# Retention and two MLPs on one core: chunks of the two sequences by turns, weights spilled in their two parts, order read from a table

## The chip, the cores and the metric

The kernel runs on one NeuronCore of a Trainium2 chip. The metric is the device time of one execution in microseconds (us), lower is better. A difference of some 0.3% is about what can be told from none. The engines are named as in the profile: PE (matmuls; PEld are its weight loads), DVE (vector), ACT (scalar), POOL (GpSimd), SP (which issues all DMAs here).

## What is computed

A retention layer (linear attention with a decay for each head) over two sequences of 768 tokens, then two MLPs over all 1536 tokens, in float32:

```python
# q, k, v: (2, 8, 768, 64)
for t in range(S):
    state = gamma * state + outer(k[:, :, t], v[:, :, t])
    y[:, :, t] = scale * q[:, :, t] @ state
x = y as (1536, 512)
h = x @ w_in                      # 512 -> 2048
P = a[0] + a[1]*h + a[2]*h**2 + a[3]*h**3
Q = 1.0 + abs(b[0])*abs(h) + abs(b[1])*h**2
x = (P / (Q + 1e-6)) @ w_out      # 2048 -> 512
h = x @ w2_in
out = (h / (1 + exp(-h))) @ w2_out
```

## The kernel before

**Parts instead of float32.** PE multiplies fp32r numbers, so each operand is held as a high part and a low part (`xh` and `xl`, `ih` and `il`, `oh` and `ol`, `gh` and `gl`), and each product is three matmuls: high by high, high by low, low by high. A weight comes in as raw words; for each unit (128 x 512) ACT makes two rows (`wt<-raw`, `raw<-raw,par`), DVE two (`wt<-wt,raw`, `wt<-raw,wt`; L371 and L373), which give the whole number in a `wt` buffer, of which there are five. From it ACT takes the high part (`ih<-wt` or `oh<-wt`, L370 in the profile), and POOL or DVE the low part (`il<-wt,ih` or `ol<-wt,oh`, L375). There are three `raw` buffers.

**Attention in twelve chunks** of 128 tokens, function `attention`. Four chunks make a token group of 512; there are three groups. The chunks stand sequence after sequence: chunks 0 to 5 are the first sequence, 6 to 11 the second, and the state `bd` goes from each chunk to the next, from one of two buffers to the other. PE makes scores (L417), the outputs (L462, and L472 from the state) and the step of the state (L450); DVE masks the scores (`am<-`) and makes `xl`; POOL multiplies keys by their decay (`kn<-kn,cst`) and queries by `gq` (`qT<-qT,gq`), which is loaded anew for ten of the chunks. All outputs of chunks 0 to 3 go through PSUM bank `h1`, so that PE's next output waits until ACT's `xh` and DVE's `xl` have read the one before.

**Steps.** A weight pair is 256 hidden features: four units of input weights and output weights in a slot. Each pair is used by two steps: 12 matmuls into a bank `h0` or `h1` (L508), an elementwise stage on ACT and DVE, a split into `gh` and `gl`, and 12 matmuls into the banks `acc` (L558). There are 96 steps: three groups by eight pairs by two, in the first MLP and in the second. Uses of a pair are counted u0 to u47, steps s0 to s95. The first MLP's elementwise stage takes six rows of DVE and five of ACT for a step, the second's one on each.

**Slots and spills.** Four slots, and two more once attention has given its memory back, hold the pairs in use. Eight pairs are needed again after their slot has gone to another: u0 to u3 come back as u20 to u23, two of the second MLP's come back as u38 and u39, two as u46 and u47. For these each whole unit goes from its `wt` to DRAM (`spill<-wt`, 32 transfers of 256 KB), comes back into a `wt` (`wt<-spill`), and is then split again by ACT (L370) and POOL or DVE (L375).

**What sets the order.** Every engine operation is recorded with a rank worked out from the numbers in `R` (due times and offsets). `Flow.order` then walks a plan with assumed durations and on each engine picks the ready operation of lowest rank; the instructions of each engine, and SP's list of DMAs, are fixed in that order. Every engine works through its list strictly in order: an instruction that waits holds all behind it, and so does a DMA on SP whose source or destination isn't ready.

Of the kernel before, what the change touches and what calls it, by code (L numbers as in the profile page):

```python
# [1 line left out]

# [5 lines left out]
F32 = mybir.dt.float32  # L8
# [11 lines left out]
R = {'T0': 321.15, 'tau0': 7.46, 'tau1': 48.5, 'c0': -178.03, 'dc': 40.95, 'conv': 16.72, 'half': 117.82, 'absl': -3.34, 'raw': 149.99, 'ret': 721.79, 'spl': 159.79, 'hi': 3.19, 'lo': -120.86, 'inn': 327.86, 'later': 56.09, 'split': 40.22, 'out': 153.78, 'evac': -230.82, 'qload': 1.4, 'scl': 120.62, 'sc': 68.71, 'am': -21.97, 'gr': 164.55, 'av': -289.58, 'bd': -408.25, 'xh': -7.59, 'xl': 65.69, 'glp': 21, 'lop1': 16, 'lop2': 24, 'scp': 0, 'ps': 18, 'ksc': 24.5, 'ka': 0, 'late': 15, 'mid': 4, 'pev': -94.54, 'pld': 38.1, 'wm': 11, 'mk': -0.34, 'ck': 14.22, 'g2': (1, 0, 2), 'lw': -276.76}  # L20
# [22 lines left out]
class Flow:  # L43
# [14 lines left out]
    def op(self, eng, dur, rank, emit, reads=(), writes=(), port=False):  # L58
        after = []
        for c in reads:  # L60
            after += c.writers
        for c in writes:
            after += c.writers + c.readers
        o = Op(eng, dur, rank, emit, list(dict.fromkeys(after)), port)
        for c in reads:
            c.readers.append(o)
        for c in writes:
            c.writers, c.readers = [o], []
        o.index = len(self.ops)
        self.ops.append(o)  # L70
        return o

    def order(self):
        free = {e: 0.6 for e in (*self.TAIL, "sync")}
        cands, done = {e: [] for e in free}, []
        port = 0.0
        landed = 0.0
        for o in self.ops:
            if not o.waits:
                cands[o.eng].append(o)  # L80
        while True:
            best = None
            for e, cs in cands.items():
                if cs:
                    at = max(free[e], min(max(o.ready, port) if o.port else o.ready for o in cs))
                    if best is None or at < best[0]:
                        best = (at, e)
            if best is None:
                break
            at, e = best  # L90
            o = min(
                (o for o in cands[e] if (max(o.ready, port) if o.port else o.ready) <= at + 1e-9),
                key=lambda o: (o.rank, o.index),
            )
            cands[e].remove(o)
            o.start = at
            if e == "sync":
                free[e] = at + self.ISSUE
                landed = max(at + self.FIRST, landed) + o.dur
                end = landed + 0.1  # L100
            else:
                free[e] = at + o.dur
                end = at + o.dur + self.TAIL[e]
            if o.port:
                port = at + o.dur
            o.end = end
            for f in o.feeds:
                f.ready = max(f.ready, end)
                f.waits -= 1
                if not f.waits:  # L110
                    cands[f.eng].append(f)
            done.append(o)
        assert len(done) == len(self.ops)
        return done
# [3 lines left out]
def retention_two_mlps(  # L118
# [104 lines left out]
    def at_chunk(c):  # L223
        return 5.5 * c if c < CPG else T0 + R["c0"] + R["dc"] * (c - CPG)

# [48 lines left out]
    bank = {n: Buf(n, [P, GT], F32, psum) for n in ("a0", "a1", "acc0", "acc1", "acc2", "acc3", "h0", "h1")}  # L274

# [56 lines left out]
    def weights(u):  # L332
        (l, p), s, old = loads[u]
        sl = slots[s]
        need = at_step[2 * u]
        for half in range(2):
            w = w_dram[l][half].bitcast(I32)
            nm = "io"[half]
            for un in range(2):
                rank = need - R["conv"] + R["half"] * half + un  # L340
                us = slice(un * UNIT, (un + 1) * UNIT)
                wt = wts()
                kept = spill.get(((l, p), half, un))
                if old:
                    dma(need - R["ret"] + half, 0.66, wt.t, kept.t, [kept], [wt])
                else:
                    raw = raws()
                    rh, rl = raw.words
                    if half == 0:
                        src = w[2 * P * un : 2 * P * (un + 1), 4 * P * p : 4 * P * (p + 1)]  # L350
                    else:
                        src = w[(2 * p + un) * P : (2 * p + un + 1) * P, :]
                    c = 2 - half
                    dst = raw.t[:].rearrange("p (c f) t -> p c (f t)", c=c)
                    dma(need - R["raw"] + half, 1.32, dst, src.rearrange("(c p) f -> p c f", p=P), [], [rh, rl])
                    wi = wt.t.bitcast(I32)
                    lo_w, hi_w = raw.t[:, :, 0], raw.t[:, :, 1]

                    act(rank - R["absl"], wt.t, hi_w.bitcast(F32), AF.Abs, [rh], [wt], more=0.03, scale=W_SCALE)

                    act(rank - R["lw"], lo_w, lo_w.bitcast(U32), AF.Identity, [lbc], [rl], ptrs=1, more=0.03, scale=L_SCALE, bias=lb)
                    stt(rank, wi, wi, 3, lo_w, ALU.logical_shift_left, ALU.bitwise_or, [rl], [wt])

                    stt(rank, wi, hi_w, -0x80000000, wi, ALU.bitwise_and, ALU.bitwise_or, [rh], [wt])
                    if kept:
                        dma(need + R["spl"], 0.66, kept.t, wt.t, [wt], [kept])
# [13 lines left out]
                op("pool" if on_pool else "dve", 1.23 if on_pool else 0.6, rank + R["lo"], lo, [wt, ch], [cl], True)  # L380


    def attention(c, s_banks, o_banks):
        b, ci = divmod(c, NCI)
# [59 lines left out]
        new = bd[c % 2]  # L444
# [53 lines left out]
    def step(s, l, g, u, j, first, last, part):  # L498
# [43 lines left out]
        for m in range(4):  # L542
# [44 lines left out]
            elif last:  # L587
# [9 lines left out]
                r0 = g * GT + m * P  # L597
# [120 lines left out]
```

## Time and profile before

| | before |
|---|---|
| median of 3 runs | 618.96 us (618.27 to 619.92) |
| the profiled execution | 618.69 us, span 616.9 us |
| PE busy | 587.8 us (95%) |
| DVE busy | 441.3 us (72%) |
| ACT busy | 388.9 us (63%) |
| POOL busy | 98.2 us (16%) |
| DMA | 71.34 MB, mean 116 GB/s |

The span is what the profiler shows from the first to the last instruction; the execution's own time lies 1.8 us above it. Matmuls are pipelined and their ends are modelled: a matmul of 512 columns shows 0.39 us, while the next begins 0.227 us later. So a busy PE is not a full one, and the stages are better judged by the number of matmuls in them.

### The profile page before, as it was taken

The numbers are of one execution on the slowest core, as the hardware profiler recorded it, in microseconds if no ns is written. First come the engines' busy times: TensorE is split into PE (matmuls) and PEld (weight loads), VectorE is DVE, ScalarE is ACT, GpSimd is POOL, SyncE is SP. The second block draws the span as 40 slices with busy tenths as digits, with TensorE's granted clock in tenths as the row PEclk, the third lists the DMA queues.
The fourth block names the chain that finished last, engine by engine and source line by source line (L and its number), as shares of the span: only waits on it lengthen the run. The fifth ranks groups of instructions, "written<-read, shape, count | busy, mean of one in ns | idle before, by whom it ended". The sixth has DMA issues, their size and how long they took to land.

```text
span 616.9 us, 8056 instructions
## 1 busy us (share of the span) xinstructions
PE 587.8 (95%) x2950; PEld 477.2 (77%) x2950; DVE 441.3 (72%) x674; ACT 388.9 (63%) x657; POOL 98.2 (16%) x80
## 2 busy tenths in 40 slices
PE   6689989999989999999999999999999999999997
PEld 6577767677768788788787877877888888888886
DVE  1788998999999999999999898985424133332321
ACT  1568878898899787879788588874333132432222
POOL 1753654455443100000000000000000000000000
PEclk8988989999989999999999999999999999999999
DMA  8996774442342211004201545684122000020001
GB/s 282 384 359 210 269 255 146 156 128 75 100 150 86 70 52 35 34 1 142 98 0 52 165 156 188 208 265 162 51 86 64 6 0 26 23 73 1 0 2 68
DMA packets 34088, 71.34 MB, mean 116 GB/s; under 512 B 3712, under 2 KB 3712, under 8 KB 34048
## 3 DMA queue, kind: packets, MB, share of 16 engines
q1 hardware_dynamic: 34048, 70.82, 34.8%
q8 instruction: 23, 0.38, 0.2%
q14 instruction: 17, 0.14, 0.1%
HBM read 58.22 MB, written 12.58 MB: 115 GB/s over the span
## 4 chain that ended last, share of the span: by engine, by line
PE 32%; DVE 15%; ACT 9%; DMA 6%; issue 3%; ACTq 0%; DVEq 0%; SPq 0%
PE acc L558 17%; PE h L508 15%; DMA raw<-in_moe_w_out_dram 3%; DMA raw<-in_moe_w_in_dram 3%; DVE wt L308 2%; DVE s L308 2%; ACT r L293 2%; DVE gl L301 2%; DVE u L308 2%; DVE r L308 1%; DVE t L308 1%; ACT w L293 1%; ACT wt L293 1%; ACT s L293 1%; ACT gh L293 1%
## 5 line engine op out<-in xcount | busy, mean ns | idle before, releaser
L508 PE MATMUL h<-xh,ih 128*128 128x512 f32 x384 | 153.6, 400 | 7.1 <-DVE s L308 5.9
L508 PE MATMUL h<-xh,il 128*128 128x512 f32 x384 | 150.8, 393 | 0.3 <-DVE il L375 0.3
L508 PE MATMUL h<-xl,ih 128*128 128x512 f32 x384 | 150.5, 392 | 0.0
L301 DVE TENSOR_TENSOR gl<-w,gh 128x512 fp32r<-128x512 f32 x48 | 33.2, 691 | 104.4 <-ACT gh L293 104.4
L293 ACT ACTIVATE gh<-w 128x512 fp32r<-128x512 f32 x48 | 30.3, 631 | 104.4 <-PE acc L558 104.4
L508 PEld LDWEIGHTS h<-xh,ih 128*128 128x128 f32 x384 | 72.7, 189 | 30.2 <-DVE s L308 12.7
L508 PEld LDWEIGHTS h<-xh,il 128*128 128x128 f32 x384 | 72.5, 189 | 17.1 <-DVE il L375 1.6
L508 PEld LDWEIGHTS h<-xl,ih 128*128 128x128 f32 x384 | 72.7, 189 | 14.3
L558 PE MATMUL acc<-gh,oh 128*128 128x512 f32 x192 | 76.3, 397 | 0.0
L558 PE MATMUL acc<-oh,gh 128*128 128x512 f32 x192 | 74.8, 390 | 0.8 <-DVE xl L301 0.8
L558 PE MATMUL acc<-gl,oh 128*128 128x512 f32 x192 | 75.0, 391 | 0.0
L558 PE MATMUL acc<-gh,ol 128*128 128x512 f32 x192 | 75.0, 391 | 0.0
L558 PE MATMUL acc<-ol,gh 128*128 128x512 f32 x192 | 74.7, 389 | 0.0
L558 PE MATMUL acc<-oh,gl 128*128 128x512 f32 x192 | 74.7, 389 | 0.0
L308 DVE SCALAR_TENSOR_TENSOR wt<-raw,wt 128x512 int32<-128x512 int32 x64 | 53.6, 845 | 0.3
L308 DVE SCALAR_TENSOR_TENSOR wt<-wt,raw 128x512 int32<-128x512 int32 x64 | 46.9, 744 | 9.1 <-ACT raw L293 8.1
L293 ACT ACTIVATE wt<-raw 128x512 f32<-128x512 f32 x64 | 42.5, 667 | 16.7 <-DMA raw<-in_moe_w_in_dram 8.4
L293 ACT ACTIVATE raw<-raw,par 128x512 int32<-128x512 uint32 x64 | 48.4, 761 | 5.0 <-DMA raw<-in_moe_w_in_dram 3.3
L308 DVE SCALAR_TENSOR_TENSOR s<-s,par,h 128x512 f32<-128x512 f32 x66 | 48.9, 743 | 0.9
L308 DVE SCALAR_TENSOR_TENSOR w<-w,h 128x512 f32<-128x512 f32 x48 | 33.0, 687 | 19.2 <-ACT w L293 18.4
L558 PEld LDWEIGHTS acc<-oh,gh 128*128 128x128 f32 x192 | 36.0, 187 | 8.7 <-DVE xl L301 1.2
L558 PEld LDWEIGHTS acc<-gh,oh 128*128 128x128 f32 x192 | 36.3, 189 | 7.9
(88 smaller groups left out, 921.6 us busy)
## 6 DMA issues: line engine op xcount, KB each, us to landing
raw<-in_moe_w_in_dram SPq DMA_DIRECT2D x32, 512.0 KB, 4.0
raw<-in_moe_w_out_dram SPq DMA_DIRECT2D x32, 512.0 KB, 3.9
spill<-wt SPq DMA_DIRECT2D x32, 256.0 KB, 4.8
wt<-spill SPq DMA_DIRECT2D x32, 256.0 KB, 2.7
kT<-in_kt_dram SPq DMA_DIRECT2D x12, 256.0 KB, 5.6
qT<-in_qt_dram SPq DMA_DIRECT2D x12, 256.0 KB, 4.7
vn<-in_v_dram SPq DMA_DIRECT2D x12, 256.0 KB, 5.2
kn<-in_k_dram SPq DMA_DIRECT2D x10, 256.0 KB, 5.5
```

The source lines that it names most:

```text
L293: lambda: nc.scalar.activation(out=out_, in_=in_, func=func, **kw),
L301: op(eng, dur, rank, lambda: e.tensor_tensor(out=out_, in0=in0, in1=in1, op=alu), reads, writes, port)
L308: lambda: nc.vector.scalar_tensor_tensor(out=out_, in0=in0, scalar=scalar, in1=in1, op0=op0, op1=op1),
L508: nc.tensor.matmul(h.t, sl.t[w][:, ws], x[g].t[:, c, :], start=(n == 0), stop=(n == 3 * KD - 1))
L558: nc.tensor.matmul(a.t, a1, a2, start=(first and n == 0), stop=(last and n == 2))
```

## The change

Three things are changed in the code, and with them the order of nearly everything.

1. Chunks take turns between the sequences: `ci, b = divmod(c, B)` instead of `b, ci = divmod(c, NCI)`. A token group now has two chunks of each sequence, each sequence has a state buffer of its own, and the factor `gq` is loaded once for the two chunks that share it (five loads instead of ten). The rows of the output go to their places accordingly.
2. A pair that is needed again is spilled from its slot as the four parts `ih`, `il`, `oh`, `ol` (32 transfers of 512 KB), and comes back as parts straight into the slot that will use it. Nothing is split a second time: 32 rows of L370 on ACT and 32 of L375 on DVE are gone.
3. The order isn't planned any more but read from a table of places (`ORDER`); `R` has other numbers too. Through these, the low parts of u24 to u29 (24 rows) and `gl` of four steps move from DVE to POOL, and the keys of chunks 0 to 3 are multiplied by ACT (8 short instructions for each) instead of POOL.

```diff
-    def order(self):
-        free = {e: 0.6 for e in (*self.TAIL, "sync")}
...
+        places = np.frombuffer(zlib.decompress(base64.b85decode("".join(ORDER))), np.uint16)
+        done = [self.ops[n] for n in places]
...
     spill = {
-        (key, h, un): Buf(f"spill{key[0]}{key[1]}{h}{un}", [P, UNIT], F32, dram)
...
+        (key, n): Buf(f"spill{key[0]}{key[1]}{n}", [P, 2 * UNIT], F32, dram) for key in sorted(again) for n in PARTS
     }
...
+        if old:
+            for n in PARTS:
+                kept = spill[(l, p), n]
+                op(
+                    "sync",
+                    1.32,
+                    need - R["ret"] + R["half"] * (n[0] == "o"),
+                    lambda n=n, kept=kept: nc.sync.dma_start(out=sl.t[n].bitcast(F32), in_=kept.t),
+                    [kept],
+                    [sl.cells[n, 0], sl.cells[n, 1]],
+                )
+            return
...
-                if old:
-                    dma(need - R["ret"] + half, 0.66, wt.t, kept.t, [kept], [wt])
...
-                    if kept:
-                        dma(need + R["spl"], 0.66, kept.t, wt.t, [wt], [kept])
...
+            if (l, p) in again:
+                for n in (nm + "h", nm + "l"):
+                    kept = spill[(l, p), n]
+                    op(
+                        "sync",
+                        1.32,
+                        need + R["spl"],
+                        lambda n=n, kept=kept: nc.sync.dma_start(out=kept.t, in_=sl.t[n].bitcast(F32)),
+                        [sl.cells[n, 0], sl.cells[n, 1]],
+                        [kept],
+                    )
...
     def attention(c, s_banks, o_banks):
-        b, ci = divmod(c, NCI)
+        ci, b = divmod(c, B)
...
-        old = bd[(c - 1) % 2]
+        old = new = bd[b]
         if more:
 
-            gq = load(0.5, gqs, decays[ci - 1])
+            gq = shared[ci] if ci in shared else load(0.5, gqs, decays[ci - 1])
+            shared[ci] = gq
...
-                r0 = g * GT + m * P
+                ci, b = divmod(g * CPG + m, B)
+                r0 = (b * NCI + ci) * P
```

Three places of the order show what moves. In the names the last number only tells buffers apart.

DVE at the start, before: from the second half of chunk 3's masked scores to `xl0` of chunk 2 (`wt` rows are the conversion of u0's weights, `bd` the steps of the state).

```order
L301 TENSOR_TENSOR w_1_135<-a1_150,msk_64 128x512
L301 TENSOR_TENSOR bd1_161<-h0_155,bd0_160 64x4x64
L308 SCALAR_TENSOR_TENSOR wt_1_128<-raw_1_125,wt_1_128 128x512
L308 SCALAR_TENSOR_TENSOR wt_2_129<-wt_2_129,raw_2_126 128x512
L308 SCALAR_TENSOR_TENSOR wt_2_129<-raw_2_126,wt_2_129 128x512
L301 TENSOR_TENSOR bd0_160<-h0_155,bd1_161 64x4x64
L301 TENSOR_TENSOR xl0_69<-h1_156,xh0_66 128x4x128
```

The same place now, on to chunk 4's scores:

```order
L312 TENSOR_TENSOR w_1_135<-a1_150,msk_64 128x512
L312 TENSOR_TENSOR u2_1_133<-a0_149,msk_64 128x512
L319 SCALAR_TENSOR_TENSOR wt_2_129<-raw_2_126,wt_2_129 128x512
L319 SCALAR_TENSOR_TENSOR wt_0_127<-wt_0_127,raw_0_124 128x512
L319 SCALAR_TENSOR_TENSOR wt_0_127<-raw_0_124,wt_0_127 128x512
L312 TENSOR_TENSOR xl0_69<-h1_156,xh0_66 128x4x128
L312 TENSOR_TENSOR am0_175<-a0_149,msk_64 128x512
L312 TENSOR_TENSOR bd0_160<-h0_155,bd0_160 64x4x64 x2
L312 TENSOR_TENSOR am1_176<-a1_150,msk_64 128x512
```

Of the conversion's rows seven stood between `xl0` of chunk 0 and that of chunk 3, and four stand there now: two have gone ahead of chunk 0's, one behind chunk 3's. On PE, the output of chunk 4 now stands ahead of the first step's matmuls instead of behind them.

The end of POOL's list, before: the last low part (`ol0`) is that of u11, and nothing comes after it.

```order
L301 TENSOR_TENSOR gl_1_147<-s1_1_137,gh_1_144 128x512
L301 TENSOR_TENSOR gl_2_148<-s1_2_138,gh_2_145 128x512
L301 TENSOR_TENSOR gl_0_146<-s1_0_136,gh_0_143 128x512
L375 TENSOR_TENSOR ol0_75<-wt_1_128,oh0_74 128x512
L714 UNCONDITIONAL_BRANCH
```

Now, from the last rows of u25 on:

```order
L392 TENSOR_TENSOR ol0_75<-wt_4_131,oh0_74 128x512
L392 TENSOR_TENSOR ol0_75<-wt_3_130,oh0_74 128x512
L392 TENSOR_TENSOR il4_1313<-wt_0_127,ih4_1312 128x512
L392 TENSOR_TENSOR ol4_1315<-wt_2_129,oh4_1314 128x512
L392 TENSOR_TENSOR il4_1313<-wt_1_128,ih4_1312 128x512
L392 TENSOR_TENSOR ol4_1315<-wt_3_130,oh4_1314 128x512
L392 TENSOR_TENSOR il5_1317<-wt_0_127,ih5_1316 128x512
L392 TENSOR_TENSOR il5_1317<-wt_4_131,ih5_1316 128x512
```

The 24 low parts of u24 to u29 have come to POOL's end; on DVE only the eight of u30 and u31 are left.

SP around the first weights that come back, before: a returning unit (`wt<-spill`) stands between the loads of u11.

```order
L327 DMA raw_1_125<-in_moe_w_in_dram 128x2x512
L327 DMA raw_1_125<-in_moe_w_out_dram 128x1024
L327 DMA wt_3_130<-spill0001_89 128x512
L327 DMA raw_2_126<-in_moe_w_in_dram 128x2x512
L327 DMA raw_0_124<-in_moe_w_out_dram 128x1024
L327 DMA wt_2_129<-spill0000_88 128x512
```

Now, the end of the eight parts of u20 and u21 (slots 4 and 5), and the loads behind them:

```order
L354 DMA il5_1317<-spill01il_93 128x1024
L354 DMA ih5_1316<-spill01ih_92 128x1024
L354 DMA ol4_1315<-spill00ol_91 128x1024
L354 DMA oh4_1314<-spill00oh_90 128x1024
L354 DMA oh5_1318<-spill01oh_94 128x1024
L354 DMA ol5_1319<-spill01ol_95 128x1024
L338 DMA raw_2_126<-in_moe_w_out_dram 128x1024
L338 DMA raw_0_124<-in_moe_w_in_dram 128x2x512
```

The parts of u20 and u21 now stand in one block ahead of the loads of three of u10's four units and of all of u11's.

## Rows read from the trace of the kernel before

**Rows 1.** The page, busy us of each engine, share of the span, instructions.

```profile
PE 587.8 (95%) x2950; PEld 477.2 (77%) x2950; DVE 441.3 (72%) x674; ACT 388.9 (63%) x657; POOL 98.2 (16%) x80
```

**Rows 2.** Stages: from:to, length, each engine's busy us (rows), PE clock, DMA share.

```profile
core 0: us, PE busy (x) PEld busy (x) DVE busy (x) ACT busy (x) POOL busy (x), PEclk, DMA share, GB/s
0.00:36.00 36.00, 24.71 (x271) 21.86 (x272) 18.79 (x31) 13.02 (x24) 16.38 (x18) 0.91 0.96 342
36.00:103.00 67.00, 61.86 (x432) 49.30 (x431) 62.51 (x93) 53.64 (x91) 34.03 (x27) 0.95 0.72 245
103.00:180.60 77.60, 72.05 (x377) 56.47 (x377) 73.11 (x105) 67.29 (x116) 38.26 (x28) 0.98 0.37 120
180.60:423.00 242.40, 238.88 (x1036) 192.75 (x1034) 228.85 (x363) 197.50 (x333) 9.58 (x7) 1.00 0.34 108
423.00:613.40 190.40, 190.34 (x837) 156.86 (x837) 58.00 (x85) 56.90 (x97) 0.00 (x0) 1.00 0.10 32
613.40:616.90 3.50, 0.00 (x0) 0.00 (x0) 0.00 (x0) 0.58 (x1) 0.00 (x0) 1.00 0.63 237
```

**Rows 3.** The chain that ended last, in order of time: start, us, what.

```profile
431.48 5.44 PE h L508 x24
597.71 15.65 PE acc L558 x69
```

**Rows 4.** Timeline of PE: start, us, engine line op, idle before.

```profile
35.78 0.50 PE L508 MATMUL h<-xh,ih 128*128 128x512 f32 x1 [0.55 <-DVE xl L301]
...
38.72 1.09 PE L462 MATMUL a<-am,vn 128*64 128x128 f32 x16
...
40.66 0.48 PE L508 MATMUL h<-xh,ih 128*128 128x512 f32 x1
```

**Rows 5.** Timeline of DVE in the first 36 us.

```profile
15.51 0.69 DVE L301 TENSOR_TENSOR xl<-h,xh 128x512 fp32r<-128x512 f32 x1 [0.81 <-ACT xh L293]
...
27.69 1.65 DVE L308 SCALAR_TENSOR_TENSOR wt<-raw,wt 128x512 int32<-128x512 int32 x1
...
32.08 1.34 DVE L308 SCALAR_TENSOR_TENSOR wt<-wt,raw 128x512 int32<-128x512 int32 x1
34.71 0.42 DVE L301 TENSOR_TENSOR bd<-h,bd 64x256 f32<-64x256 f32 x1 [1.29 <-PE h L450]
35.05 0.67 DVE L301 TENSOR_TENSOR xl<-h,xh 128x512 fp32r<-128x512 f32 x1
```

**Rows 6.** Groups of instructions, whole span: busy us, mean ns of one, idle before.

```profile
L370 ACT ACTIVATE ih<-wt 128x512 fp32r<-128x512 f32 x48 | 29.9, 626 | 9.3 <-DVE wt L308 6.0 <-PE h L508 2.9
L375 DVE TENSOR_TENSOR il<-wt,ih 128x512 fp32r<-128x512 f32 x32 | 22.9, 721 | 3.3 <-ACT ih L370 3.1
L375 DVE TENSOR_TENSOR ol<-wt,oh 128x512 fp32r<-128x512 f32 x32 | 22.0, 686 | 1.4 <-ACT oh L370 1.3
L301 POOL TENSOR_TENSOR gl<-s,gh 128x512 fp32r<-128x512 f32 x22 | 30.3, 1376 | 32.1 <-ACT gh L293 22.4 <-issue 7.2 <-POOL gl L301 2.2
L375 POOL TENSOR_TENSOR il<-wt,ih 128x512 fp32r<-128x512 f32 x16 | 21.4, 1338 | 31.8 <-ACT ih L370 31.5
L617 ACT ACTIVATE par<-par 128x1 f32<-128x1 f32 x1 | 0.2, 187 | 0.0
```

**Rows 7.** DVE's conversion rows from 0 to 213 us, while POOL works.

```profile
L308 DVE SCALAR_TENSOR_TENSOR wt<-raw,wt 128x512 int32<-128x512 int32 x32 | 31.8, 1004 | 0.2
L308 DVE SCALAR_TENSOR_TENSOR wt<-wt,raw 128x512 int32<-128x512 int32 x32 | 25.0, 800 | 3.9 <-ACT raw L293 3.8
```

**Rows 8.** The same from 213 to 423 us, while POOL is idle.

```profile
L308 DVE SCALAR_TENSOR_TENSOR wt<-wt,raw 128x512 int32<-128x512 int32 x32 | 21.8, 689 | 5.2 <-ACT raw L293 4.3 <-ACT wt L293 0.9
L308 DVE SCALAR_TENSOR_TENSOR wt<-raw,wt 128x512 int32<-128x512 int32 x32 | 21.8, 687 | 0.1
```

**Rows 9.** The page, DMA issues: count, KB each, median us to landing.

```profile
raw<-in_moe_w_in_dram SPq DMA_DIRECT2D x32, 512.0 KB, 4.0
spill<-wt SPq DMA_DIRECT2D x32, 256.0 KB, 4.8
```

**Rows 10.** Waits: SP's queue from 36 to 135 us: us, times, longest.

```profile
SPq L327 <- DVE wt L308: 55.4, 15, 7.4
```

**Rows 11.** Waits of POOL from 36 to 103 us.

```profile
POOL il L375 <- ACT ih L370: 13.4, 5, 5.0
```

**Rows 12.** Timeline, SP's last input-weight load of u3 and PE's first matmul of step 6.

```profile
76.53 0.38 SPq L327 DMA_DIRECT2D raw<-in_moe_w_in_dram  x1
...
90.01 0.39 PE L508 MATMUL h<-xh,ih 128*128 128x512 f32 x1
```

More of the change, by code (lines that the diff above doesn't have):

```diff
@@ L1 @@
+import base64
+import zlib
 from contextlib import ExitStack
+import numpy as np
 import concourse.bass as bass
@@ L64, in op @@
         o = Op(eng, dur, rank, emit, list(dict.fromkeys(after)), port)
+        banks = [c.bank for c in (*reads, *writes) if c.bank is not None]
+        o.bank = banks[0] if banks and eng in ("act", "dve") else None
         for c in reads:
@@ L73, in order @@
     def order(self):
-        free = {e: 0.6 for e in (*self.TAIL, "sync")}
[L75 to L113, printed above, removed]
+        places = np.frombuffer(zlib.decompress(base64.b85decode("".join(ORDER))), np.uint16)
+        assert sorted(places) == list(range(len(self.ops)))
+        done = [self.ops[n] for n in places]
+        for n, o in enumerate(done):
+            o.place = n
+        assert all(o.place < f.place for o in done for f in o.feeds)
         return done
@@ L223, in at_chunk @@
     def at_chunk(c):
-        return 5.5 * c if c < CPG else T0 + R["c0"] + R["dc"] * (c - CPG)
+        return R[f"ch{c}"] + (5.5 * c if c < CPG else T0 + R["c0"] + R["dc"] * (c - CPG))
     cst = Buf("cst", [P, NGAM])
@@ L339, in weights @@
             for un in range(2):
-                rank = need - R["conv"] + R["half"] * half + un
+                rank = need - R["conv"] + early + R["half"] * half + un
                 us = slice(un * UNIT, (un + 1) * UNIT)
                 wt = wts()
-                kept = spill.get(((l, p), half, un))
-                if old:
-                    dma(need - R["ret"] + half, 0.66, wt.t, kept.t, [kept], [wt])
-                else:
[L347 to L364, printed above, removed]
-                    if kept:
-                        dma(need + R["spl"], 0.66, kept.t, wt.t, [wt], [kept])
@@ new lines, in weights @@
+                raw = raws()
+                rh, rl = raw.words
+                if half == 0:
+                    src = w[2 * P * un : 2 * P * (un + 1), 4 * P * p : 4 * P * (p + 1)]
+                else:
+                    src = w[(2 * p + un) * P : (2 * p + un + 1) * P, :]
+                c = 2 - half
+                dst = raw.t[:].rearrange("p (c f) t -> p c (f t)", c=c)
+                dma(need - R["raw"] + R.get(f"lu{u}", 0.0) + half * R["rhalf"], 1.32, dst, src.rearrange("(c p) f -> p c f", p=P), [], [rh, rl])
@@ new lines, in weights @@
+                wi = wt.t.bitcast(I32)
+                lo_w, hi_w = raw.t[:, :, 0], raw.t[:, :, 1]
+                act(rank - R["absl"], wt.t, hi_w.bitcast(F32), AF.Abs, [rh], [wt], more=0.03, scale=W_SCALE)
+                act(rank - R["lw"], lo_w, lo_w.bitcast(U32), AF.Identity, [lbc], [rl], ptrs=1, more=0.03, scale=L_SCALE, bias=lb)
+                stt(rank, wi, wi, 3, lo_w, ALU.logical_shift_left, ALU.bitwise_or, [rl], [wt])
+                stt(rank, wi, hi_w, -0x80000000, wi, ALU.bitwise_and, ALU.bitwise_or, [rh], [wt])
```

56 lines of the change are left out of this document (47 added, 9 removed).

## Prediction

> **What bounds the kernel now.** I read the page's busy times first [rows 1]: PE is busy 95% of the span, DVE 72%. Since a busy PE isn't a full one, I take the spacing of its matmuls from the chain of waits: 24 matmuls in 5.44 us, 0.2267 us each [rows 3]. Then I read the busy times by stage [rows 2]. They fall into three regimes.
>
> From 423.0 to 613.4 us PE has 837 matmuls, 837 x 0.2267 = 189.7 of 190.4 us. Nothing but fewer matmuls could shorten this, and the change removes none. DVE is busy 30% here.
>
> From 180.6 to 423 us it has 1036 of them, 234.8 of 242.4 us: 7.6 us are lost, 3.5 of them as plain idle time. DVE is busy 228.9 us (94%), ACT 81%.
>
> Up to 180.6 us PE is idle 11.3 + 5.1 + 5.6 = 22.0 us, and the granted clock, 0.91, 0.95 and 0.98, takes away about 3.2 + 3.4 + 1.6 = 8 us more. DVE is busy 93 to 94% from 36 us on. At the very start it is not the amount of work that counts but a chain: the first step's matmuls begin at 35.78 us, when DVE has written chunk 3's `xl` [rows 4, 5]. Chunk 0's `xl` began at 15.51, chunk 3's at 35.05. In between DVE worked through conversion rows of up to 1.65 us each which stood ahead of the `xl` rows that PE waited for.
>
> So the change can gain in two places: the start, and the middle stage with its 7.6 us. What it does after 423 us is hidden by PE.
>
> **The change part by part.** All sums are made against the profiled execution, 618.69 us, which lies 0.27 under the median.
>
> *The start.* Of DVE's conversion rows between chunk 0's and chunk 3's `xl`, seven become four, and the state of chunk 2 no longer waits for that of chunk 1 but only for chunk 0's. How soon could the first step start? Up to chunk 3's `v`, SP's list holds 27 pieces of 256 KB (7.08 MB) before and after; at 342 GB/s, the mean of the stage [rows 2], that is 20.7 us, and with some 2 us before the first data 22.7. Then come PE's output (38.72 to 40.66, 1.94 us [rows 4]), `xh` and `ih` on ACT (0.63 each [rows 6]), and POOL's `il` (1.34 [rows 6]): 27.2, and with semaphores and a little queueing 29 us. The other end is 35.8, no gain. Chunk 4's output now stands ahead of the first step, so PE has 2 us more behind it at that moment. The gain is between 35.8 - 29 + 2.2 = 9.0 and 0. Of this DVE decides how much is kept, since it stays at 94%: ahead of its first row of step 18 I count 224 rows in the order before and 223 now, so no work has left this stretch, it can only begin sooner. I take half, **4.5 us**.
>
> In the same stretch ACT gets 4 x 8 short rows for the keys. The trace has none of this shape: between 0.19 (128x1) and 0.63 us (128x512) [rows 6], 6 to 20 us; the small end is nearer to 64 columns, 1.5 to 2 us a chunk. ACT was busy 13.0 of the first 36 us [rows 2], and that room covers it; without it each would push an `xh`, and so PE, by up to 2 us. The five `gq` loads that are dropped save 1.3 MB, 3.8 us of DMA at 342 GB/s, but most of that comes after the first step. I count nothing for either.
>
> *No second split.* 16 of the 32 removed low parts lie between 180.6 and 423 us, on DVE: 16 x 0.69 (0.721 and 0.686 [rows 6]) = 11.0 us. The other 16 lie behind 423 us and are worth nothing. ACT loses 16 x 0.63 = 10 us in the middle too.
>
> *24 low parts and four `gl` from DVE to POOL.* 28 x 0.69 = 19.3 us leave DVE. POOL takes 28 x 1.35 = 38 us [rows 6] in a stage in which it was busy 9.6 of 242 us [rows 2]. But beside a working POOL DVE's conversion rows are slower: 1004 and 800 ns on the mean up to 213 us, 687 and 689 after it [rows 7, 8]; 32 x (0.317 + 0.111) = 13.7 us over POOL's 74 operations, 0.19 us for each. 28 more cost 5 us by the mean, and up to 28 x (1.65 - 0.69) = 27 us if each one met a row at its worst [rows 5, 8].
>
> DVE's busy time in the middle is then 228.9 - 11.0 - 19.3 + 5 = 204 us, 84% instead of 94: its room grows from 13.5 to 39 us. Against that stand PE's 7.6 lost us. With three times the room I expect the waits for DVE to shrink to some 3 us, as the stage behind loses 0.7 with DVE at 30%. I take **4.5 us**; the ends are 0 and 7.6.
>
> *Bigger spills.* 32 transfers of 256 KB each way become 32 of 512 KB [rows 9], 8.4 MB more each way, 25 us of DMA at 342 GB/s in each direction. The writes fall mostly between 36 and 140 us, where DMA is busy 72 and 37%, the returns where it is 34% and less [rows 2]. A return must now wait until its slot is free, but the slots of u22, u23 and of the last four are free some ten steps (54 us) before their use, against 5 us of landing. Nothing, by that cover; if it went, PE would wait for a whole landing.
>
> *SP's list.* The block of eight returns ahead of the loads of u10 and u11 waits for the end of attention (chunk 11's output, on PE now 2.7 us later in the steps), then needs 4.2 MB, 12 us. Step 14, beside which DVE's first conversion of u10 stands, is some 20 us behind that output: nothing, with a few us to spare.
>
> Sum: 618.7 - 4.5 - 4.5 = **609.7 us**, 1.5% less.
>
> **The rivals.** *Both gains whole.* The start comes at its bound (9.0), the middle is as full as the end (7.0), time 602.7; and the idle time between 36 and 180 us may shrink with it, to 599. For it speaks that an order was fixed for exactly this work; against it that DVE has as many rows ahead of step 18 as before.
>
> *POOL's rows hold DVE's.* The low parts on POOL meet conversion rows that read two operands from SBUF, as at 27.69 us, where one took 1.65 instead of 0.69 [rows 5, 8]. At the worst end DVE's 30 us are given back but 3, the middle keeps its 7.6, and the time is 618.7 - 4.5 = 614.2. The Trainium skill speaks for it (SBUF — State Buffer, "Who interferes with whom"): a vector instruction with two SBUF inputs and a GpSimd instruction that reads SBUF take the same port, and one blocks wholly; and in Perfetto Trace Analysis, "Optimizing Scalar/DVE Operations", moving work between the two might not help. By that rule, 614.2; the trace agrees on the mechanism (1.65 against 0.69), but not on its frequency, 0.19 us for each of POOL's operations.
>
> *A spill holds SP's list; slower.* The first four pairs' 16 parts stand in SP's list among the loads of u3, u8 and u9, and each waits until both units are in the slot, so the eight low ones wait for POOL. Before, a spill needed only DVE's conversion, and SP still waited 55.4 us for such rows, up to 7.4 at once [rows 10]. Now `ih` (0.63), POOL's wait (13.4 / 5 = 2.7 [rows 11]) and its row (1.34) come on top, 4.7 us for each, 37 in all. It decides where a hold is longer than what the loads behind it have to spare: u3's last input load was issued at 76.53 and used at 90.01 [rows 12], 13.5 us, of which landing (4.0 [rows 9]), ACT, DVE, ACT and POOL need about 9. If half the holds stand there, PE loses 37 / 2 - 4.4 = 14 us: 624. Against it: these parts stand late in the list, for pairs converted long before.
>
> *The change brings nothing*, since PE's losses in the middle come from chains within a step and not from DVE's load: 618.7, or a little under.
>
> **How the numbers follow.** Forecast (606 to 614) 0.50; both gains whole 0.15; POOL holds DVE 0.13; SP held, slower 0.14; nothing 0.08. The range leaves out the slower case and little else: 599 to 618.5. About 0.3% can be told from no change here, so faster means under 617.1: 0.50 + 0.15 + 0.13, and a little off for ends that reach across, 0.77; slower, above 620.8, 0.14; the same 0.09.
>
> **What would show it.** Right: the first `h<-xh,ih` at 30 to 33 us; DVE busy some 84% between PE's start of step 20 and step 64, and that stretch 4 to 5 us shorter than 240; the last 190 us unchanged. Wrong at the start: that first matmul at 35 us or later, or DVE idle in the first 100 us for loads. The port: `wt<-raw` in the middle well over 0.8 us. SP: holds of over 5 us at a `spill<-` ahead of `raw<-`, and PE idle just behind. What would make it wrong altogether is a wait in a list that nothing in the trace of before shows, since every engine's order has been written anew.

## The result and the profile after

The changed kernel takes **601.59 us** (median of 4 runs, 599.60 to 602.01) against 618.62 of the kernel before on the same chip: ratio 0.9715, interval 0.9688 to 0.9741. That is 17 us or 2.8% less; the forecast was 609.7, the range 599.0 to 618.5. The profiled execution took 602.01 us, its span is 600.2.

Busy time of each engine after, the line that answers to [rows 1]:

```profile
PE 579.1 (96%) x2950; PEld 475.0 (79%) x2950; DVE 409.2 (68%) x614; ACT 378.7 (63%) x657; POOL 137.3 (23%) x104
```

And by stage, as in [rows 2], but cut where PE starts the first step, step 8, step 20 and step 64 (30.4, 97.1, 171.8 and 410.6 us):

```profile
0.00:30.40 30.40, 24.41 (x287) 21.44 (x287) 15.79 (x29) 20.10 (x55) 8.71 (x13) 0.94 0.93 315
30.40:97.10 66.70, 59.66 (x446) 47.26 (x443) 62.43 (x98) 53.90 (x91) 36.87 (x29) 0.97 0.79 269
97.10:171.80 74.70, 71.91 (x364) 57.81 (x364) 67.77 (x101) 68.19 (x117) 39.52 (x28) 1.00 0.64 228
171.80:410.60 238.80, 237.25 (x1042) 194.99 (x1041) 217.35 (x320) 189.20 (x317) 52.21 (x35) 1.00 0.38 128
410.60:596.70 186.10, 185.83 (x820) 153.53 (x818) 45.89 (x68) 46.95 (x79) 0.00 (x0) 1.00 0.17 60
```

The stages hold other numbers of matmuls than before (1042 here from step 20 to 64, 1027 before), so their lengths can't be compared as they stand. For this I use one measure throughout: **lost time**, the moment at which PE begins its n-th group of 12 input matmuls, less what all PE work ahead of that moment takes at its bare spacing (0.2267 us for a step's matmul [rows 3], 1.09 us for a chunk's scores, 0.6 for its state, 0.98 and 0.96 for its output, 0.23 for each of the 22 matmuls on `u` ahead of the first chunk). Both kernels have the same matmuls, so the differences in lost time add up to the difference in time:

| PE time lost, us | before | after | gained |
|---|---|---|---|
| up to the first group | 15.5 | 9.1 | 6.4 |
| 1st to 5th (before 36 to 70 us) | 6.5 | 10.6 | -4.1 |
| 5th to 21st (70 to 183) | 15.2 | 6.0 | 9.2 |
| 21st to 49th (183 to 332) | 3.3 | 1.1 | 2.2 |
| 49th to 65th (332 to 423) | 4.4 | 1.7 | 2.7 |
| after that | 0.6 | 0.1 | 0.5 |
| sum | 45.5 | 28.6 | 16.9 |

So 11.5 us come from the first 183 us, 4.9 from the middle, and 0.5 from the end. In the first stretch one profile isn't exact: four kernels below (e1, e2, e10, e11) have the same code up to step 20 as the kernel after, and lose 17.1 to 20.1 us up to the 5th group; from the 5th to the 21st all five agree within 0.4 us (6.0 to 6.4).

The start after, PE's first step and DVE's rows of that time (start, us, then the instruction), which answer to [rows 4, 5]:

```profile
30.39 0.50 PE L538 MATMUL h<-xh,ih 128*128 128x512 f32 x1
```

```profile
15.66 0.69 DVE L312 TENSOR_TENSOR xl<-h,xh 128x512 fp32r<-128x512 f32 x1 [0.52 <-ACT xh L304]
...
28.91 0.69 DVE L312 TENSOR_TENSOR xl<-h,xh 128x512 fp32r<-128x512 f32 x1
```

Chunk 0's `xl` stands where it stood (15.51 before); from it to chunk 3's it is now 13.3 us instead of 19.5.

Then, PE's idle time behind the first step. The larger waits before, up to step 20:

```profile
47.24 1.09 PE L462 MATMUL a<-am,vn 128*64 128x128 f32 x16 [2.04 <-DVE am L301]
...
62.67 1.16 PE L417 MATMUL a<-qT,kT 64*128 64x128 f32 x16 [0.57 <-ACT bd L293]
...
81.06 0.69 PE L450 MATMUL a<-vn,kn 128*64 128x64 f32 x16 [2.14 <-DVE am L301]
...
112.38 1.16 PE L417 MATMUL a<-qT,kT 64*128 64x128 f32 x16 [0.53 <-DVE bd L301]
...
116.76 1.09 PE L462 MATMUL a<-am,vn 128*64 128x128 f32 x16 [0.94 <-DVE am L301]
...
173.41 0.50 PE L508 MATMUL h<-xh,ih 128*128 128x512 f32 x1 [1.95 <-DVE s L308]
```

and after:

```profile
39.50 1.09 PE L492 MATMUL a<-am,vn 128*64 128x128 f32 x16 [0.91 <-DVE am L312]
...
43.85 1.16 PE L447 MATMUL a<-qT,kT 64*128 64x128 f32 x16 [1.56 <-DVE bd L312]
...
47.70 1.12 PE L480 MATMUL a<-vn,kn 128*64 128x64 f32 x16 [2.69 <-DVE am L312]
...
68.66 0.50 PE L538 MATMUL h<-xh,ih 128*128 128x512 f32 x1 [0.47 <-DVE s L319]
...
138.94 0.50 PE L538 MATMUL h<-xh,ih 128*128 128x512 f32 x1 [0.61 <-DVE s L319]
...
151.30 0.50 PE L538 MATMUL h<-xh,ih 128*128 128x512 f32 x1 [1.16 <-DVE s L319]
...
163.50 0.50 PE L538 MATMUL h<-xh,ih 128*128 128x512 f32 x1 [1.02 <-DVE s L319]
```

The waits inside attention, for the state `bd` or the masked scores `am`, have moved rather than gone: together they are 6.5 us before, from 47 to 133 us, and 6.2 after (1.0 of it a wait whose releaser the profile doesn't show), all of them ahead of 48 us. That is what the stretch from the 1st to the 5th group gives back. From the 5th to the 21st group, attention's waits go from 3.9 us to nothing, and the steps' waits for `s` from 3.8 to 2.8. That stretch before and after (the second number is PE's busy time, the third from the end its mean granted clock, with 1.00 for the upper level of 2.4 GHz):

```profile
69.92:182.64 112.72, 105.03 (x578) 82.98 (x578) 105.73 (x152) 94.91 (x161) 53.67 (x41) 0.97 0.44 144
```

```profile
68.66:171.83 103.17, 100.38 (x551) 80.50 (x552) 95.37 (x145) 93.25 (x160) 54.36 (x40) 1.00 0.67 236
```

Idle time gives 4.9 of the 9.2 us there (7.7 before, 2.8 after). The clock gives 3.4: before, it fell twice in this stretch, and after, not at all. One such place before, two slices of 6 us:

```profile
168.00:174.00 6.00, 4.05 (x19) 3.03 (x18) 5.36 (x10) 5.69 (x11) 1.34 (x2) 1.00 0.51 181
174.00:180.00 6.00, 6.00 (x21) 4.75 (x20) 5.26 (x7) 5.06 (x10) 3.91 (x3) 0.72 0.45 133
```

PE stood 2 us idle, and in the slice behind that it was granted less, which cost 1.7 us. Behind the first step, such a fall follows the waits at 47, 81 and 173 us in the kernel before, and only the pair at 44 and 48 us in the kernel after. Taken together, the 1st to the 21st group have 10.7 us of idle time before and 9.8 after, but lose 5.1 us to the clock before and 1.7 after: of the 5.1 us that this whole stretch gains, the larger part is clock. Of the 6.4 us up to the first group, 1.7 are clock as well.

### The profile page after: what moved, and what is told of

It reads as the page before. It is cut to its first block, busy times and chain, and to the rows that moved or that the text cites. A ratio compares the mean times of both kernels' runs of the same rounds, so it can differ in the third digit from the quotient of the medians.

```text
span 600.2 us, 7998 instructions
## 1 busy us (share of the span) xinstructions
PE 579.1 (96%) x2950; PEld 475.0 (79%) x2950; DVE 409.2 (68%) x614; ACT 378.7 (63%) x657; POOL 137.3 (23%) x104
## 4 chain that ended last, share of the span: by engine, by line
PE 70%; DVE 13%; DMA 8%; ACT 5%; issue 2%; SPq 1%; ACTq 0%; DVEq 0%
PE h L538 34%; PE acc L588 32%; DMA raw<-in_moe_w_in_dram 4%; DVE wt L319 3%; DVE s L319 3%; DMA raw<-in_moe_w_out_dram 2%; DVE s L312 1%; DVE u L319 1%; DVE t L319 1%; DMA spill03oh<-oh 1%; SPq L338 1%; ACT raw L304 1%; DMA kT<-in_kt_dram 1%; DVE r L319 1%; DVE gl L312 1%
## 5 line engine op out<-in xcount | busy, mean ns | idle before, releaser
L538 PE MATMUL h<-xh,ih 128*128 128x512 f32 x384 | 150.9, 393 | 5.2 <-DVE s L319 4.2
L538 PE MATMUL h<-xl,ih 128*128 128x512 f32 x384 | 149.6, 390 | 0.0
L312 DVE TENSOR_TENSOR gl<-w,gh 128x512 fp32r<-128x512 f32 x48 | 34.8, 725 | 110.6 <-ACT gh L304 109.9
L538 PEld LDWEIGHTS h<-xh,il 128*128 128x128 f32 x384 | 72.1, 188 | 15.2
L538 PEld LDWEIGHTS h<-xl,ih 128*128 128x128 f32 x384 | 72.1, 188 | 14.6
L392 POOL TENSOR_TENSOR il<-wt,ih 128x512 fp32r<-128x512 f32 x28 | 39.5, 1415 | 97.0 <-ACT ih L387 89.4
L392 POOL TENSOR_TENSOR ol<-wt,oh 128x512 fp32r<-128x512 f32 x28 | 42.6, 1527 | 44.0 <-ACT oh L387 41.6
L319 DVE SCALAR_TENSOR_TENSOR wt<-raw,wt 128x512 int32<-128x512 int32 x64 | 52.0, 819 | 0.4
L304 ACT ACTIVATE wt<-raw 128x512 f32<-128x512 f32 x64 | 42.5, 669 | 15.2 <-DMA raw<-in_moe_w_in_dram 8.8
L312 POOL TENSOR_TENSOR gl<-s,gh 128x512 fp32r<-128x512 f32 x26 | 35.3, 1362 | 66.4 <-ACT gh L304 32.1
```

What stands on the lines that cost most here:

```text
L304: lambda: nc.scalar.activation(out=out_, in_=in_, func=func, **kw),
L312: op(eng, dur, rank, lambda: e.tensor_tensor(out=out_, in0=in0, in1=in1, op=alu), reads, writes, port)
L319: lambda: nc.vector.scalar_tensor_tensor(out=out_, in0=in0, scalar=scalar, in1=in1, op0=op0, op1=op1),
L392: e.tensor_tensor(out=sl.t[nm + "l"][:, us], in0=wt.t, in1=sl.t[nm + "h"][:, us].bitcast(F32), op=ALU.subtract)
L538: nc.tensor.matmul(h.t, sl.t[w][:, ws], x[g].t[:, c, :], start=(n == 0), stop=(n == 3 * KD - 1))
```

## The experiments

Two theories go in. The **room** theory is the prediction's: PE loses time in the middle because DVE is full, so whatever takes rows from DVE (POOL, no second split) gains. The **order** theory: each engine's list, as fixed now, carries the gain, and the parts could be undone or done alone with little effect. In these kernels each operation keeps its place in the common list of the kernel it is made from; of the operations whose inputs are there, the one with the lowest place comes next. Ratios are to the kernel before on the same chip; after has 0.9715.

| kernel | ratio (95% interval) | lost to 1st | 1st-5th | 5th-21st | 21st-49th | 49th-65th |
|---|---|---|---|---|---|---|
| before | 1 | 15.5 | 6.5 | 15.2 | 3.3 | 4.4 |
| after | 0.9715 (0.9688-0.9741) | 9.1 | 10.6 | 6.0 | 1.1 | 1.7 |
| e1 after, 28 rows back on DVE | 0.9718 (0.9689-0.9747) | 9.4 | 8.9 | 6.0 | 2.4 | 0.8 |
| e2 after, split again | 0.9829 (0.9793-0.9866) | 9.9 | 8.5 | 6.2 | 9.4 | 1.4 |
| e10 after, split again, DVE only | 0.9861 (0.9825-0.9898) | 9.6 | 10.5 | 6.4 | 8.7 | 1.9 |
| e11 after, weights later | 0.9908 (0.9877-0.9939) | 9.2 | 7.9 | 6.1 | 5.6 | 8.8 |
| e3 after, keys on POOL | 0.9702 (0.9661-0.9743) | 9.5 | 11.2 | 6.8 | 1.9 | 2.1 |
| e4 after, chunks in sequence | 0.9949 (0.9919-0.9979) | 18.1 | 13.9 | 10.2 | 1.3 | 2.5 |
| e9 after, ten `gq` loads | 0.9767 (0.9732-0.9801) | 11.4 | 8.3 | 6.8 | 1.6 | 2.6 |
| e5 after, planned order | 1.0339 (1.0300-1.0378) | 24.0 | 6.9 | 14.7 | 12.4 | 7.7 |
| e6 before, 28 rows on POOL | 1.0065 (1.0042-1.0088) | 14.6 | 8.2 | 14.5 | 3.7 | 8.4 |
| e7 before, direct returns | 1.0086 (1.0054-1.0117) | 15.9 | 6.6 | 15.6 | 1.9 | 7.3 |
| e8 before, three parts | 1.0214 (1.0187-1.0241) | 14.4 | 15.1 | 16.7 | 1.6 | 9.5 |
| e12 before, direct and early | 1.0478 (1.0435-1.0521) | 14.2 | 10.6 | 14.7 | 26.3 | 5.1 |

### e1: the rows on POOL

```diff
-R = {..., 'glp': 25, 'lop2': 30, ...}
+R = {..., 'glp': 21, 'lop2': 24, ...}
```

> The kernel after, with its order as it is, but the low parts of u24 to u29 (24 rows) and gl of s22 to s25 (4 rows) are again on DVE, at the places where POOL had them. In the kernel after, DVE is busy 217.4 of 238.8 us between the starts of steps 20 and 64 (91%), and PE loses 2.8 us there against a spacing of 0.2267 us. If DVE's room is what the middle gained by: 28 x 0.69 = 19.3 us come back and some 10 us of stretching beside POOL go, DVE stands at 95% or more, PE's loss rises to 5 to 8 us, and the time to 604 to 607. If the order of the rows is what counts: no more than 1 us, 601 to 602.6.

Measured 603.03 us, the same ratio as after. The room theory wanted 604 to 607. DVE's conversion rows between steps 20 and 64, after and then e1 (busy us, mean ns), and below them that stage of e1 (DVE's busy time is the fourth number):

```profile
L319 DVE SCALAR_TENSOR_TENSOR wt<-raw,wt 128x512 int32<-128x512 int32 x35 | 29.1, 835 | 0.3
L319 DVE SCALAR_TENSOR_TENSOR wt<-wt,raw 128x512 int32<-128x512 int32 x34 | 25.9, 765 | 1.0 <-ACT raw L304 0.8
```

```profile
L381 DVE SCALAR_TENSOR_TENSOR wt<-raw,wt 128x512 int32<-128x512 int32 x35 | 23.8, 686 | 0.2
L381 DVE SCALAR_TENSOR_TENSOR wt<-wt,raw 128x512 int32<-128x512 int32 x34 | 23.2, 686 | 1.2 <-ACT raw L366 1.1
```

```profile
170.50:409.70 239.20, 237.83 (x1043) 194.97 (x1042) 221.01 (x348) 189.70 (x318) 10.19 (x7) 1.00 0.38 128
```

28 rows more, 19.3 us of work, and DVE is busy 221.0 us instead of 217.4: moving them to POOL frees 3.7 us of DVE, since the rows that stay get longer. The conversion rows (835 instead of 686 ns, 765 instead of 686) make up some 8 us of this, and DVE's `gl`, `s` and `r` rows some 5 more. PE hardly notices: e1 loses 1.3 us more up to the 49th group and 0.9 less behind it.

### e2 and e10: the second split

e2 puts a copy on ACT and a row on DVE on each returned unit, in place; e10 only the row on DVE.

```diff
+            for half, un in ((0, 0), (0, 1), (1, 0), (1, 1)):
...
+                flow.put = PLACE[f"st_{2 * u - 2 + half}__0"] + 0.1 * un
+                op("act", ..., lambda ...: nc.scalar.activation(out=sl.t[n][:, us], in_=sl.t[n][:, us].bitcast(F32), func=AF.Copy), [], [ch])
+                op("dve", ..., lambda ...: nc.vector.tensor_tensor(out=sl.t[n][:, us], in0=..., in1=..., op=ALU.max), [ch], [cl])
```

> The kernel after, with its order as it is, plus 32 rows on ACT and 32 on DVE: each returned unit is written once more in place, two steps before its use, a copy of the high part on ACT (0.63 us) and a row of two SBUF inputs on DVE (0.69 us) on the low part. The results are the same. 16 of each lie between steps 20 and 64: 11 us of DVE, 10 us of ACT. If DVE's room is what the middle gained by: DVE goes from 91 to 95%, PE's loss there from 2.8 to 5 or 7 us, the time to 603.5 to 606. If the order counts: 601 to 602.6.

> The kernel after plus only the 32 DVE rows of the run that splits returned units again, without the 32 rows on ACT. In that run PE lost 7.2 us between its 37th and its 49th input step, where DVE went from 65.7 of 68.5 to 74.2 of 74.8 us. If DVE is the bound there: 16 x 0.6 = 9.6 us less the 2.8 us that DVE was idle, 6 to 7 us again, 607 to 609. If ACT or the two in turn held it: 1 to 4 us, 602.5 to 605.5.

609.06 and 609.04 us: about 7 and 9 us by ratio. For e2 that is more than the room theory said; for e10 it is what was expected if DVE is the bound. Without ACT's rows the loss is the same within the intervals. Nearly all of it is lost between the 37th and the 49th group. That stretch after, in e2 and in e10 (DVE's busy time is the fourth number), and what PE waits for there in e10:

```profile
252.00:318.50 66.50, 65.92 (x290) 53.93 (x289) 63.69 (x100) 55.93 (x93) 8.77 (x6) 1.00 0.39 133
```

```profile
250.90:325.70 74.80, 67.22 (x290) 53.59 (x289) 74.16 (x116) 64.08 (x109) 9.88 (x6) 1.00 0.34 119
```

```profile
252.00:326.00 74.00, 68.47 (x290) 54.76 (x289) 73.67 (x116) 55.78 (x94) 9.49 (x6) 0.98 0.36 124
```

```profile
PE h L628 <- DVE s L381: 5.4, 3, 1.9
```

DVE was at 63.7 of 66.5 us; the 16 rows use up nearly all of the 2.8 us that it had and lengthen the stretch by the rest. In e10 a fall of the clock (0.98) comes on top, 1.7 us. Here DVE is the bound, as the prediction had it; of e1's 28 rows only six stood in this stretch (POOL's 8.8 us in the first line), and most behind it, where DVE has 82%.

### e11: weights ready later

e11 changes only the table: the places of load, conversion and spill of u25 to u31 are each 30 higher.

> The kernel after, but loads, conversion and spills of u25 to u31 stand 30 places later in the common order (some 6 to 8 us). In the kernel after, the input weights of u26 to u31 are ready 1.8 to 6.7 us before their step, in the kernel before -1.8 to 0.2 us, and PE loses 1.7 and 4.4 us between the 49th and the 65th input step. If being ready ahead is what the table gained there: the lead goes to about 0 or below, PE loses 5 to 10 us there, and the time is 605 to 610. If it is something else, since DVE has as much to do as before: within 1.5 us of 601.6.

611.96 us, 12 us more by ratio and just above the range that was expected if the lead counts, with no operation more or less and nothing moved from one engine to another. How long the input weights are complete before their step (end of the unit's last `il` to the step's first matmul), us:

| | u25 | u26 | u27 | u28 | u29 | u30 | u31 |
|---|---|---|---|---|---|---|---|
| before | 0.7 | 0.2 | -0.8 | -0.4 | -0.4 | -0.9 | -1.8 |
| after | 14.9 | 6.7 | 5.3 | 3.9 | 6.2 | 2.2 | 1.8 |
| e7 | 0.7 | -0.8 | -0.8 | -0.4 | -0.7 | -0.8 | -3.0 |
| e11 | 7.6 | -1.7 | -1.3 | -1.7 | -1.6 | -1.3 | -0.1 |
| e12 | 20.5 | 13.5 | 9.3 | 6.6 | 6.2 | 3.7 | 2.3 |

A step begins while its last low part is still in work, so a negative lead means that PE may be held, not that it is. For u28 in e11, POOL's last low part and PE's first matmul, a place where PE isn't held:

```profile
372.96 1.30 POOL L456 TENSOR_TENSOR il<-wt,ih 128x512 fp32r<-128x512 f32 x1 [2.46 <-ACT ih L451]
```

```profile
372.57 0.39 PE L622 MATMUL h<-xh,ih 128*128 128x512 f32 x1
```

The loss from the 49th to the 65th group goes from 1.7 to 8.8 us. PE's waits in that stretch in e11, in the kernel before, and after:

```profile
PE h L622 <- ACT ih L451: 2.5, 2, 2.2
PE acc L672 <- DVE xl L374: 1.7, 1, 1.7
PE h L622 <- POOL il L456: 0.6, 1, 0.6
```

```profile
PE h L508 <- DVE s L308: 0.9, 1, 0.9
PE acc L558 <- DVE xl L301: 0.8, 1, 0.8
PE h L508 <- DVE il L375: 0.3, 1, 0.3
```

```profile
PE h L538 <- DVE w L319: 1.0, 1, 1.0
```

Of e11's loss, 3.1 us are waits for weights (`ih`, `il`), and 1.7 are a fall of the clock behind them (0.98 on the mean). (4.5 us more are lost in the eight groups ahead of that, whose own weights were back long before: the moved rows disturb what they now stand beside, too.) So without its lead the stretch loses a lot more, with as much for DVE to do. But the lead is not shown to be the whole of the 2.7 us that the kernel after gains over the one before here: before, the weights' part is some 1.5 of the 4.4 us, if the waits too short for the list are counted in, and `s` and `xl` have 2.2. DVE is also less busy in this stretch, 82% of the time after and 90% before, and no run separates the two.

### e6, e7, e8 and e12: the parts in the old order

e6 has `lop2` 30 and `glp` 25; e7 the direct spills and returns of the change's diff, each spill right behind its low parts, each return where its first unit came back; e8 both, and the alternating chunks with shared `gq`. e12 is e7 with loads and conversions of u24's output weights to u31 15 to 60 places earlier, and the second MLP's spills 45 places later.

> The kernel before, with its order as it is, but the low parts of u24 to u29 and gl of s22 to s25 (28 rows) on POOL at the places where DVE had them. If DVE's room sets the loss in the middle: DVE from 94 to some 90%, PE's loss of 7.8 us there falls by 2 to 4, the time 614.5 to 616.5. If the order counts: within 1 us of 618.6, or up to 2 us slower, since POOL's row takes 1.35 to 1.6 us where DVE's took 0.69 and what waits for it comes later.

> The kernel before, with its order as it is as far as the dependencies allow, but spills and returns are the four parts from and to the slots, so that 32 rows each on ACT and DVE are gone. If DVE's room sets the loss in the middle: 11 us less of DVE there, 94 to 89%, and 1.5 to 4 us less time, 614.5 to 617. If the order counts: 617.5 to 620; if a part now holds SP's list ahead of the loads: slower, up to 624.

> The kernel before, with its order as it is as far as the dependencies allow, and three parts of the change at once: alternating chunks with shared gq, direct spills and returns, 28 rows on POOL. Not the table, not the keys on ACT. If the parts carry the gain: 604 to 610. If the order carries it: 615 to 622.

> The kernel before with direct spills and returns, as in the run that gave 623.8, but with the room used: loads and conversions of u24's output weights and of u25 to u31 stand 15 to 60 places earlier in the common order, and the spills of the second MLP's weights 45 places later, behind the loads that follow. If the direct returns pay only where DVE's freed rows let the next weights be ready sooner, and SP's list isn't held by their spills: the loss between the 49th and the 65th input step falls from 7.3 to 3 or 4 us, and the time is 619 to 621, with all of that 4.4 or less 617 to 619. If the parts are worth nothing in any order: 623 or more.

622.62, 623.81, 631.19 and 646.39 us: all slower than before, and e6 and e8 above both ranges that were expected. In e6 the 4 us are lost from the 49th to the 65th group, where weights have no lead and a low part now takes 1.42 to 1.52 us instead of 0.69. PE's waits there:

```profile
PE h L605 <- ACT ih L448: 1.6, 2, 1.0
PE h L605 <- POOL il L453: 1.5, 3, 0.6
```

e7 gains 1.4 us from the 21st to the 49th group, as the room theory said, and loses 2.9 behind it. (The profile is of a run of 621.25, 2.6 us above the profiled one of before, and so shows half of the 5 us.) SP's waits at spills in that stretch:

```profile
SPq L462 <- ACT oh L445: 6.3, 3, 3.7
SPq L462 <- ACT ih L445: 2.6, 3, 1.1
SPq L462 <- DVE ol L450: 1.8, 3, 0.8
SPq L462 <- DVE il L450: 1.6, 3, 0.6
```

12.3 us in all, ahead of the next raw loads, in a stretch without lead: the mechanism of the rival that was to be slower. After has as much of it (14.4 us from step 48 to 64), but a lead that covers it. That the holds are what e7 loses by isn't shown apart, since e12 moved spills and conversions together. e12's lead is 2 to 20 us, and from the 53rd to the 65th group it loses 0.6 us against 5.4 in e7; but the rows that were pulled ahead cost 24 us where they now stand:

```profile
PE h L608 <- DVE s L380: 19.2, 4, 10.2
```

### e3, e4, e5 and e9: the first 180 us

e3 sets `ka` to 0; e9 loads `gq` for each chunk; e4 does that too, and

```diff
-        ci, b = divmod(c, B)
+        b, ci = divmod(c, NCI)
...
-        old = new = bd[b]
+        old, new = bd[(c - 1) % 2], bd[c % 2]
```

e5 plans the order as the kernel before does, from the `R` of the kernel after.

> The kernel after, with its order as it is, but the keys of chunks 0 to 3 are multiplied by POOL (one row of 1.04 us each) and not by ACT (8 short rows, 2.0 us each). If the earlier first step (30.39 us against 35.78) comes from DVE's conversion rows no longer being held by POOL's: some of these rows before 30 us take 1 to 1.7 us again, the first step starts at 32 to 34 us, and 1.5 to 3 us of it are left at the end (603 to 604.6). If it comes from the two chains of states and the order on DVE: the first step within 0.7 us of 30.4, since ACT has 8 us less to do, and the time within 1 us of 601.6.

> The kernel after, with its order as it is as far as the dependencies allow, but the chunks stand sequence after sequence again, with the two state buffers by turns and ten gq loads. If the alternation carries the gain up to 180 us (11.5 us of lost PE time by step 20): chunks 1 to 3 wait for each other's states and for five more loads of 0.26 MB, the first step comes 2 to 5 us later, and the time is 606 to 612. If the order on DVE carries it: the first step 0 to 1.5 us later and the time 601.5 to 604.

> The kernel after with all its parts and its numbers in R, but the order planned as in the kernel before, and not read from the table. If the parts carry the gain, a plan with the same due times keeps most of it: 601 to 605. If the row by row order carries it: 607 to 616, with the loss spread over the start, the stage to step 20 and the middle.

> The kernel after, with its order as it is, but gq is loaded for each chunk (ten loads of 256 KB instead of five), the five extra ones halfway between their neighbours in the list. If it is DMA that cost the run with chunks in sequence its first 9 us: 1.3 MB more, 3.8 us at 342 GB/s, the first step at 32 to 36 us and the time 604 to 608. If it was the chain of states from chunk to chunk: the first step within 1 us of 30.4 and the time 601 to 603.

e3, 600.61 us: no difference (the profile is of a run of 605.02); ACT's short rows for the keys bought nothing. e9, 603.35: its first step comes at 32.7 instead of 30.4 us, and by the 5th group that is gone; its 3 us by ratio are not clear of the noise, since the intervals overlap.

e4, 616.46 (613.21 to 619.96; the profile is of a run of 619.23): first step at 40.4 us. PE at the start of e4:

```profile
17.06 2.08 PE L520 MATMUL acc<-qT,kT 64*128 64x128 f32 x16 [3.16 <-DMA kT<-in_kt_dram]
...
26.67 1.09 PE L568 MATMUL h<-am,vn 128*64 128x128 f32 x16 [2.22 <-DVE xl L374]
...
31.66 1.16 PE L520 MATMUL a<-qT,kT 64*128 64x128 f32 x16 [2.81 <-DMA qT<-in_qt_dram]
```

Its profile loses 9.0 us more by the first step, with later loads and a later `xl`; 3.3 and 4.2 us follow up to the 21st group. Much of the first two is clock: 0.83 and 0.87 on the mean up to the 1st and from there to the 5th group, where after has 0.94 and 0.96. Of the 4.2, only 1.7 stand at a wait inside attention; the rest is for `s`, at the steps. 616 us is above both expected ranges, and the order was made for the alternation. So this order without the alternation keeps only a little; what an order made for chunks in sequence would keep isn't shown. And the alternation in the old order (e8) has its first step 2.0 us sooner than before, loses 8.6 us more by the 5th group, and 1.5 more up to the 21st. Neither half carries the 11.5 us.

e5, 640.15: the same parts, planned, are 39 us slower than by the table. That is far outside both ranges. In the kernel after, the due times in `R` set no order, so e5 doesn't tell how good a plan with other numbers could be.

## Why the prediction was right, and where it was wrong

The direction was right, and the time lies in the range; the size was little more than half. The rival "both gains whole" named the right time (602.7, or 599 with less idle time from 36 to 180 us), but not for its reasons: neither gain is whole, and what it gave a passing clause, the stage from 36 to 180 us, has as large a part as the start and the middle.

**The start** (4.5 us taken, 0 to 9). The sign held: first step at 30.39, within 30 to 33, and chunk 3's `xl` comes sooner behind fewer conversion rows, as was named; no run tests these rows apart. 6.4 us are gained there, 1.7 of them clock, and 4.1 given back by the 5th group, at the waits for `am` and `bd` from 39 to 48 us, so 2.3 last. That only part is kept was said; it is half of what I took.

**36 to 180 us** is the step that failed: I carried no term for it. I had seen 22 us of idle time and 8 of clock up to 180 us, and reasoned on DVE's count of rows ahead of step 18 (224 and 223), from which nothing could shrink but the start. 9.2 us of lost time went from the 5th group on; if the 4.1 us are counted here and not at the start, the whole stage gains 5.1. Attention's waits were not shortened by much (6.5 and 6.2 us) but stand close together now, ahead of 48 us, and the clock falls once there instead of three times up to step 20, 3.4 us. What brought them together, the alternation or the other places of the new order, stays open: e4 loses 4.2 of the 9.2 again, but most of that not inside attention.

**The 28 rows on POOL.** Priced at 19.3 us less 5. DVE got 3.7 (e1): the rows beside POOL stretch by (19.3 - 3.7) / 28 = 0.56 us for each operation moved, not 0.19. The 0.19 came from conversion rows alone, and `gl`, `s` and `r` stretch too; 0.56 lies halfway to the worst row's 0.96 [rows 5, 8]. The sign that was named for it, `wt<-raw` well over 0.8 us, came out at 0.835. The rival on POOL's rows had the cause right, took too much at its worst end (27 us given back where e1 shows 15.6), and was wrong in what follows: the middle didn't keep its 7.6. The Trainium skill's sentence behind it (Perfetto Trace Analysis, "Optimizing Scalar/DVE Operations"), that moving work between the two might not help, agrees with e1.

**The middle** (4.5 taken, 4.9 measured) came out for another reason than I gave, so that the size is luck. DVE's room didn't triple: it is busy 91%, not 84%. Up to step 48 it is as full as before (141.5 of 146.7 us against 145.5 of 149.6). The 16 second splits do count (e2, e10: 7 to 9 us if they come back there), since the new order put conversions of later weights in their place: 9 or 10 units from step 20 to 48, where before had 5 or 6 (DVE's `wt` rows there). From that come the leads of 2 to 15 us, without which the stretch behind loses 7 us more (e11); how much of its gain from 4.4 to 1.7 us is the lead, and how much DVE's 82 instead of 90%, isn't shown.

**Bigger spills and SP's list** at nothing: right after, where PE's waits behind the first step name no returned part, and the holds at spills fall in a stretch with lead. In the old order, without lead, the direct returns lose more than they gain (e7), so the cover was worth a price: e7 stands 5 us above before.

**The change brings nothing** and **slower** are out. That every engine's order is written anew stood at the end, as something that could only make the forecast wrong; it had no place and no price. Most of the missing 8 us lies in a stretch where only the order and the alternation differ much, but which places earn it isn't shown.

## What to carry to other kernels

Where a change frees an engine's time, ask what the order puts into the room: the time freed is worth something only if a later piece of work is ready sooner for it, so read the lead of each input before its use and not the busy share alone. Where waits that you saw are gone, add up all that are there now: they may only have moved, and what has changed may be the clock behind them. A part of a change tried in an order made for another can be slower (the direct returns in e7, against e2 and e10; the rows on POOL in e6, against e1) though in its own order it gains or costs nothing. And a stage in which the bound engine loses time without an obvious chain still needs a term, if only a range.

## What the runs showed of the hardware

DVE's rows get longer beside POOL's (e1), and POOL's got longer too: low parts took 1.34 us (`il`) before [rows 6] and 1.42 (`il`) and 1.53 (`ol`) after, on the mean:

```profile
L392 POOL TENSOR_TENSOR il<-wt,ih 128x512 fp32r<-128x512 f32 x28 | 39.5, 1415 | 97.0 <-ACT ih L387 89.4
...
L392 POOL TENSOR_TENSOR ol<-wt,oh 128x512 fp32r<-128x512 f32 x28 | 42.6, 1527 | 44.0 <-ACT oh L387 41.6
```

DVE's busy share alone doesn't tell this: it was 93 to 94% where POOL's rows ran before [rows 2], and 91% from step 20 to 64 after, where they are longest. Which of DVE's rows they meet isn't shown apart. Both sides paid for the 24 low parts and four `gl` that moved: DVE kept 15.6 of the 19.3 us, and POOL spent 42 (52.2 - 10.2) for them between steps 20 and 64.
